# A linear-attention, mixture and maxout kernel: tile 1's loads and half of w_k moved up, the sums' writes later, first ffn mixing ahead of conversions

## The chip, the cores and the metric

The kernel runs on one core of one Trainium2 chip. The metric is the time of one execution on the device in microseconds; lower is better. The program has one launch, and all its weights and inputs are read from the chip's memory in it.

## The reference

Three stages follow one another over 3072 tokens of width 256. The first is a linear attention with a decaying state, in chunks of 32 in the reference; the second mixes each token with the one before it and runs a gated feed-forward layer; the third takes the largest of three products and projects it back.

```python
def _attn_ref(x, a, B, C):
    log_a = np.log(np.clip(a, 1e-06, 1.0))
...
    for c in range(nc):
...
        M = np.einsum('bhin,bhjn->bhij', Cc, Bc) * L
        y_intra = np.einsum('bhij,bhjd->bhid', M, xc)
        y_inter = np.einsum('bhin,bhnd->bhid', Cc, state) * decay_to_i[:, :, :, None]
        y[:, :, sl] = y_intra + y_inter
        state = decay_full[:, :, None, None] * state + np.sum(Bx, axis=2)

def _moe_ref(x, mu_k, mu_r, w_k, w_v, w_r):
...
    xk = mu_k * x + (1.0 - mu_k) * x_prev
    xr = mu_r * x + (1.0 - mu_r) * x_prev
    k = np.maximum(xk @ w_k, 0.0)
    v = k * k @ w_v
    r = 1.0 / (1.0 + np.exp(-(xr @ w_r)))
    return (r * v).astype(np.float32)

def _moe2_ref(x, w1, w2, w3, w_out):
    h = np.maximum(np.maximum(x @ w1, x @ w2), x @ w3)
    return (h @ w_out).astype(np.float32)
```

The weights come as 64-bit floats, and the kernel makes each product of a large layer as three products of split numbers (high by high, low by high, high by low).

## The kernel before

The 768 positions of four sequences are cut into six tiles of 128 positions; a tile has 512 tokens. `attention(t)` works on two chunks of 64 positions in each tile. For a tile it does the following. `inputs(t)` loads bl (B) and xt (x) and multiplies bl with a decay into bd. `gather` (L770) forms what each chunk adds to the state, from bd and xt; `heads` masks it into um. `cb` (L856) makes the scores of C (cw) and B (bt), which VectorE multiplies with the decays in L. `carried` (L881) multiplies the state with ce and `yt` (L891) the scores with xt, both into the accumulators pb0 and pb1. Copies of these into xb (L929) end the tile's attention. `sums()` makes running sums of log a for all tiles with L599, copies them on ScalarE (L603 as they are, L604 through exp), and writes them to memory as crd and ced, from where later tiles read the rows L and ec that `decays` and the state need. For tiles 0 and 1 the decays are spread on TensorE instead (L716 to L724).

`gate(t)` mixes xb with the token before it (L961, L962, L964), splits the result into k2h and k2l (L413 and L421, the high and the low part) and multiplies with w_r (L982), and `ffn(t)` mixes with the other weights into xk00h, xk00l, xk01h and xk01l, multiplies with w_k in eight groups of six products (L1005), squares the positive part on ScalarE (evacuations L1011, L1012, L1014), and multiplies with w_v (L1026). `maxout` (L686 on) and `final` follow for the tile before.

`load_split` brings a block of 64-bit weights: one DMA, an Abs on ScalarE (L629), four bit operations on VectorE (L630 to L636), a copy of the high part and a subtraction for the low part. wrh, wrl, wkh, wkl, wvh and wvl are the results. The first half of w_k comes as two blocks, the second half as one into h2, converted by way of wol.

What sets the order is the class `Plan`. Every operation is entered with a cost, its readers and writers, and a `bias`; a list scheduler in the kernel's own Python simulates the five engines 60 times with urgencies taken from the last round, and `issue()` writes each engine's instructions in the order of the best round. An engine works its list strictly in order. All loads go through one list, SyncE's. `first` adds to the bias of a DMA alone, `after` names operations that must come before. The planner has constants for what it knows of the chip: FETCH, BLOCK and FRONT say when TensorE's next block of instructions is there, EARLY is a number of very narrow matmuls (L1165) put ahead of all work, and WARM rules fillers (L1163) between.

## Time and profile before

| what | us |
|---|---|
| runs | 414.48, 414.15, 410.01 |
| median | 414.15 |
| profiled execution | 413.59 |
| its span, from first to last instruction | 411.9 |
| TensorE busy | 400.0 |
| VectorE busy | 254.8 |
| ScalarE busy | 215.3 |
| GpSimd busy | 62.3 |

The mean granted clock of TensorE is 0.987 of the full one. The chain of work that ended last runs through TensorE for 83% of the span, through VectorE for 8%, ScalarE 4%, DMA 2%, and "issue" (time in which an engine waits for nothing that the profile shows) 2%. Matmul lengths in the timeline overlap the next ones: in a row of 128x512 products one starts 0.23 us after another, whatever their listed lengths say. Line numbers of the profile are those of the kernel before; in the changed kernel they are 1 to 6 higher.

### The profile page before, as it was taken

How to read it: one execution, taken by the hardware profiler on the slowest of the kernel's cores; microseconds unless marked ns; L12 is line 12 of the kernel's file. 1: busy time of each engine (PE TensorE's matmuls, PEld its weight loads, DVE VectorE, ACT ScalarE, POOL GpSimd, SP SyncE). 2: the span in 40 equal slices, each digit the busy share in tenths (PEclk: the TensorE clock that was granted, in tenths of full speed). 3: DMA queues.
4: the chain of work that ended last, by engine and by line, in shares of the span. 5: the costliest groups of instructions: out<-in, count | busy, mean ns of one | idle time of the engine just before them, and what ended most of it. 6: DMA issues, size and time to landing. Idle time of an engine off the chain costs nothing.

```text
span 411.9 us, 8673 instructions
## 1 busy us (share of the span) xinstructions
PE 400.0 (97%) x3687; PEld 320.8 (78%) x3687; DVE 254.8 (62%) x413; ACT 215.3 (52%) x379; POOL 62.3 (15%) x63
## 2 busy tenths in 40 slices
PE   9797999999999999999999999999999999999996
PEld 6565777878877888787888888888887888888885
DVE  3898989999998655473664474565374224540632
ACT  5499578974476843255762154762145743222321
POOL 4104010000102340232130032140022200010010
PEclk9999799999999999999999999999999999999999
DMA  7686637560135500023300000500000000001001
GB/s 270 226 244 206 216 100 209 180 204 26 55 96 178 138 25 0 29 79 115 91 25 2 28 2 4 127 25 0 2 2 27 0 25 2 0 0 53 0 2 51
DMA packets 12879, 31.55 MB, mean 77 GB/s; under 512 B 1768, under 2 KB 4136, under 8 KB 12072
## 3 DMA queue, kind: packets, MB, share of 16 engines
q1 hardware_dynamic: 12840, 30.99, 24.3%
q8 instruction: 29, 0.48, 0.5%
q14 instruction: 10, 0.08, 0.1%
HBM read 27.64 MB, written 3.34 MB: 75 GB/s over the span
## 4 chain that ended last, share of the span: by engine, by line
PE 83%; DVE 8%; ACT 4%; issue 2%; DMA 2%; SPq 0%; ACTq 0%
PE pa L686 31%; PE pa L1026 15%; PE pa L1005 14%; PE pa L1102 9%; PE pa L982 3%; PE pb L1102 2%; PE pb L891 2%; PE pb L856 2%; DVE tmp L1064 1%; PE pb L881 1%; PE pa L701 1%; DMA bl<-in_b_l_dram 1%; PE pa L1165 1%; DVE tmp L964 1%; DMA outs<-in_w_out_dram 1%
## 5 line engine op out<-in xcount | busy, mean ns | idle before, releaser
L1064 DVE TENSOR_TENSOR tmp<-tmp,pa 128x512 f32<-128x512 f32 x72 | 49.1, 686 | 55.6 <-PE pa L686 54.6
L421 DVE TENSOR_TENSOR k2l<-tmp,k2h 128x512 fp32r<-128x512 f32 x52 | 37.5, 735 | 41.2 <-ACT tmp L1014 33.9
L413 ACT ACTIVATE hr<-tmp 128x512 fp32r<-128x512 f32 x36 | 22.7, 632 | 70.7 <-DVE tmp L1064 70.5
L1026 PE MATMUL pa<-k2h,wvh 128*128 128x512 f32 x96 | 38.2, 398 | 0.0
L1026 PE MATMUL pa<-k2h,wvl 128*128 128x512 f32 x96 | 38.0, 396 | 0.0
L1026 PE MATMUL pa<-k2l,wvh 128*128 128x512 f32 x96 | 37.8, 393 | 0.0
L1102 PE MATMUL pa<-hr,worh 128*128 128x512 f32 x120 | 37.5, 394 | 0.0
L1011 ACT ACTIVATE tmp<-pa 128x512 f32<-128x512 f32 x48 | 28.0, 593 | 13.9 <-PE pa L1005 13.6
L1062 ACT ACTIVATE tmp<-pa 128x512 f32<-128x512 f32 x36 | 21.5, 598 | 23.1 <-PE pa L686 19.4
L1012 ACT ACTIVATE k2h<-tmp 128x512 fp32r<-128x512 f32 x48 | 30.2, 632 | 2.9 <-PE pa L1026 1.6
L421 DVE TENSOR_TENSOR hr<-tmp,hr 128x512 fp32r<-128x512 f32 x28 | 19.3, 695 | 14.8 <-ACT hr L413 14.7
L421 POOL TENSOR_TENSOR hr<-tmp,hr 128x512 fp32r<-128x512 f32 x8 | 10.3, 1291 | 110.9 <-ACT hr L413 110.9
L1102 PEld LDWEIGHTS pa<-hr,worh 128*128 128x128 f32 x120 | 22.2, 188 | 5.5 <-ACT th L987 0.7
L1014 ACT ACTIVATE tmp<-tmp 128x512 f32<-128x512 f32 x37 | 23.3, 633 | 0.7
L1102 PE MATMUL pa<-hr,worl 128*128 128x512 f32 x60 | 23.4, 389 | 0.0
L1026 PEld LDWEIGHTS pa<-k2h,wvh 128*128 128x128 f32 x96 | 18.0, 188 | 4.4 <-issue 0.2
L1026 PEld LDWEIGHTS pa<-k2h,wvl 128*128 128x128 f32 x96 | 18.0, 188 | 4.3
L1026 PEld LDWEIGHTS pa<-k2l,wvh 128*128 128x128 f32 x96 | 18.0, 188 | 4.1
L1073 ACT ACTIVATE outs<-pa 128x512 f32<-128x512 f32 x9 | 5.4, 599 | 26.5 <-PE pa L1102 26.5
L964 DVE SCALAR_TENSOR_TENSOR tmp<-xb,bits,tmp 128x512 f32<-128x512 f32 x24 | 18.4, 792 | 0.7 <-ACT tmp L962 0.3
L868 DVE TENSOR_TENSOR L<-pb,L 128x512 f32<-128x512 f32 (+1 forms) x28 | 15.8, 608 | 2.7 <-ACT h L629 2.6
L1041 DVE SCALAR_TENSOR_TENSOR tmp<-th,pa 128x512 f32<-128x512 f32 x12 | 8.0, 689 | 14.5 <-PE pa L1026 14.5
(273 smaller groups left out, 986.5 us busy)
## 6 DMA issues: line engine op xcount, KB each, us to landing
h<-in_w_dram SPq DMA_DIRECT2D x6, 768.0 KB, 5.0
L<-crd SPq DMA_DIRECT2D x8, 512.0 KB, 6.6
cw<-in_c_w_dram SPq DMA_DIRECT2D x6, 512.0 KB, 4.0
xt<-in_x_l_dram SPq DMA_DIRECT2D x6, 512.0 KB, 3.5
out_dram<-outs SPq DMA_DIRECT2D x10, 256.0 KB, 2.0
h<-in_w_v_dram SPq DMA_DIRECT2D x2, 1024.0 KB, 6.0
bt<-in_b_t_dram SPq DMA_DIRECT2D x6, 256.0 KB, 4.4
bl<-in_b_l_dram SPq DMA_DIRECT2D x6, 256.0 KB, 3.5
```

The source lines that it names most:

```text
L413: A.activation(ap(out_), ap(in_), AF.Copy)
L421: op({"DVE": tt(n), "POOL": pool(n, narrow)}, 0, lambda e: (V if e == "DVE" else G).tensor_sub(ap(out_), ap(x0), ap(x1)), r=r, w=w, after= ...
L686: T.matmul(pt, l, r_, start=(i == 0), stop=(i == last))
L964: op("DVE", 61 + tt(n), lambda tv=tv, c=c: V.scalar_tensor_tensor(out=tv, in0=xb[:, c, bs, :P], scalar=om[:, i, c:c + 1], in1=tv, op0=ALU. ...
L1005: T.matmul(p.ap[:, :n], l, r_, start=(c == 0 and i == 0), stop=(c == KC - 1 and i == 2))
L1011: op("ACT", 51 + 0.833 * n, lambda: A.activation(sq, p.ap[:, :n], AF.Relu), r=[p], w=[tm])
L1012: op("ACT", act(n), lambda: A.activation(hi, sq, AF.Square), r=[tm], w=[kb])
L1014: A.activation(sq, sq, AF.Square) if e == "ACT" else
L1026: T.matmul(pv[c2].ap[:, :n], l, r_, start=(f == 0 and i == 0), stop=(f == FC - 1 and i == 2))
L1062: op("ACT", 51 + 0.833 * TW, lambda p=p, tm=tm: A.activation(tm.ap, p.ap, AF.Copy), r=[p], w=[tm])
L1064: op("DVE", tt(TW), lambda p=p, tm=tm: V.tensor_tensor(out=tm.ap, in0=tm.ap, in1=p.ap, op=ALU.max), r=[p], w=[tm])
L1102: T.matmul(p.ap, l, r_, start=(g == 0 and i == 0), stop=(g == GC - 1 and i == 2))
```

## The change

There are five edits. The planner's second FETCH entry now ends at 14.5 us with a delay of 2.8 us in place of 20 and 3.4, and EARLY is 140 where it was 118. The writes of crd get a bias that puts them behind those of ced. The first half of w_k and the mixing of the first ffn get a bias of 40000, which makes them more urgent. The second half of w_k and the loads of tile 1 (bl, xt, bt, cw) no longer follow one another by `after`: the chain was bt, w_k, cw, ct, then bl and xt, and now each of them waits for one thing, the first gather of tile 0, and ct for nothing, with biases that give them the order w_k, bl, xt, bt, cw, ct.

```diff
--- before.py
+++ after.py
@@ -91,11 +91,11 @@
     FIRST = 1500.0
     STAY = 8000.0
     BLOCK, FRONT = 128, 92
-    FETCH = ((9000.0, 5600.0), (20000.0, 3400.0), (60000.0, 3200.0), (1e9, 2600.0))
+    FETCH = ((9000.0, 5600.0), (14500.0, 2800.0), (60000.0, 3200.0), (1e9, 2600.0))
     OPEN = (1000.0, 28.0)
     HEAVY = (2100.0, 16000.0, 1300.0)
     WARM = (3400.0, 430.0, 215.0, 100.0, 600.0)
-    EARLY = 118
+    EARLY = 140
     ROUNDS = 60
     SPARE = (200.0, 1000.0)
     ENGINES = ("PE", "ACT", "POOL", "DVE", "SP")
@@ -337,6 +337,7 @@
 SPREAD = 2
 LATE = 0
 EARLY1 = -20000.0
+AHEAD = (40000.0, 40000.0)
 FIRST = (9.85e5, 9.8e5, 9.9e5, 9.83e5, 9.5e5, 9.95e5, 9.6e5)
 
 
@@ -605,7 +606,7 @@
         for s in range(2):
             dma(200, ced[s * QH:(s + 1) * QH], crow[:, s, 1], r=[b_er], w=[b_ced[s]])
             dma(200, crd[:, s * QH:(s + 1) * QH].rearrange("c q i -> q c i"),
-                crow[:, s, 0].rearrange("q (c i) -> q c i", c=2), r=[b_cr], w=[b_crd[s]])
+                crow[:, s, 0].rearrange("q (c i) -> q c i", c=2), r=[b_cr], w=[b_crd[s]], first=EARLY1)
         p = boot.bufs[2]
         op("PE", 350, lambda p=p: T.matmul(p.ap[:, :NC], tri, la, start=True, stop=True), r=[b_la, b_tri], w=[p])
         b_cc.readers = [k for s in (b_af, b_ts) for k in s.readers + s.writers]
@@ -652,18 +653,20 @@
         plan.bias = BIAS[1]
         load_split(w_r.rearrange("p (k n) -> p k n", k=KC), wr_t[0], wr_t[1], KC, CH, [b_wr], FIRST[3],
                    place=(stage.next(2 * TW), word.next(TW)))
-        plan.bias = 0.0
+        plan.bias = AHEAD[1]
         spots = [(stage.next(2 * TW), word.next(TW)), ((wo_f[0][:, :2 * TW], wide[:1]), word.next(TW)),
                  (stage.next(4 * TW), (wo_f[1][:, :2 * TW], narrow[:1]))]
         for c in range(KC):
             load_split(w_k[c * P:(c + 1) * P, None, fs[0]], wk_t[0][:, c:c + 1, fs[0]], wk_t[1][:, c:c + 1, fs[0]],
                        1, FF // 2, [b_wk[c][0]], FIRST[4] - 1.5e5 * c, place=spots[c])
-        k = dma(935, bt.rearrange("p u i -> p (u i)"), b_t[1], w=[b_bt], first=FIRST[4] - 4e5)
-        k = load_split(w_k[:, fs[1]].rearrange("(c p) n -> p c n", p=P), wk_t[0][:, :, fs[1]], wk_t[1][:, :, fs[1]],
-                       KC, FF // 2, [b_wk[c][1] for c in range(KC)], FIRST[4] - 4.5e5, place=spots[2], after=[k])
-        k = dma(1870, cw.rearrange("p u i -> p (u i)"), c_w[1], w=[b_cw], after=[k])
-        k = dma(935, ct.rearrange("p u i -> p (u i)"), c_t[1], w=[b_ct], after=[k])
-        inputs(1, after=[k])
+        plan.bias = 0.0
+        k = [begun['loads']]
+        load_split(w_k[:, fs[1]].rearrange("(c p) n -> p c n", p=P), wk_t[0][:, :, fs[1]], wk_t[1][:, :, fs[1]],
+                       KC, FF // 2, [b_wk[c][1] for c in range(KC)], FIRST[4] - 4e5, place=spots[2], after=k)
+        inputs(1, (FIRST[4] - 4.2e5, FIRST[4] - 4.3e5), after=k)
+        dma(935, bt.rearrange("p u i -> p (u i)"), b_t[1], w=[b_bt], first=FIRST[4] - 4.4e5, after=k)
+        dma(1870, cw.rearrange("p u i -> p (u i)"), c_w[1], w=[b_cw], first=FIRST[4] - 4.5e5, after=k)
+        dma(935, ct.rearrange("p u i -> p (u i)"), c_t[1], w=[b_ct], first=FIRST[4] - 4.6e5)
         for f in range(FC // 4):
             load_split(w_v[f].rearrange("p (k n) -> p k n", k=4), wv_t[0][:, 4 * f:4 * f + 4], wv_t[1][:, 4 * f:4 * f + 4], 4, CH, [b_wv[f]])
 
@@ -823,10 +826,11 @@
 
         def states(k):
             m = 32 * len(k)
-            op("PE", m * 10.8 + SWITCH * m / 64, lambda: gather(t, U, k), r=[b_bd, b_xt[t]], w=[U[c] for c in k], burst=m)
+            begun['states'] = op("PE", m * 10.8 + SWITCH * m / 64, lambda: gather(t, U, k), r=[b_bd, b_xt[t]], w=[U[c] for c in k], burst=m)
 
         if t < 2:
             states((0,) if first else (0, 1))
+            begun.setdefault('loads', begun['states'])
 
         def heads(c):
             uv = U[c].ap[:, TW // 2:].rearrange("p (b s d) -> p b s d", b=NB, s=2)
@@ -991,7 +995,9 @@
     def ffn(half, t):
         hv, cols, bs, n = tokens(half)
         xkt, b_xkt = xk_hl[t % 2], b_xk[t % 2]
+        plan.bias += AHEAD[0] * (t == 0)
         mix(0, xkt, b_xkt, half, t)
+        plan.bias -= AHEAD[0] * (t == 0)
 
         def s2(f):
             p = pm.next()
```

On SyncE's list this stood before from the load of tile 1's bt on (ced, crd: the sums; h2 and h3: weights; xt0, xt1: x of even and odd tiles):

```order
L426 DMA woh_79<-in_w_k_dram 128x1024
L426 DMA bt_115<-in_b_t_dram 128x512
L426 DMA h2_93<-in_w_k_dram 128x2x1024
L426 DMA xt0_121<-in_x_l_dram 128x1024
L426 DMA ced_82<-h0_91 96x128 x2
L426 DMA h3_94<-in_w_v_dram 128x2048
L426 DMA cw_116<-in_c_w_dram 128x1024
L426 DMA ec_119<-ced_82 128x1x512
L426 DMA ct_117<-in_c_t_dram 128x512
L426 DMA crd_81<-h0_91 96x2x64 x2
L426 DMA bl_124<-in_b_l_dram 128x512
L426 DMA xt1_122<-in_x_l_dram 128x1024
```

And now:

```order
L427 DMA woh_79<-in_w_k_dram 128x1024
L427 DMA h2_93<-in_w_k_dram 128x2x1024
L427 DMA bl_124<-in_b_l_dram 128x512
L427 DMA xt1_122<-in_x_l_dram 128x1024
L427 DMA bt_115<-in_b_t_dram 128x512
L427 DMA cw_116<-in_c_w_dram 128x1024
L427 DMA ct_117<-in_c_t_dram 128x512
L427 DMA xt0_121<-in_x_l_dram 128x1024
L427 DMA h3_94<-in_w_v_dram 128x2048
L427 DMA ced_82<-h0_91 96x128
L427 DMA crd_81<-h0_91 96x2x64
L427 DMA ced_82<-h0_91 96x128
```

bl and xt1 of tile 1 have moved from behind both writes of the sums to behind the second half of w_k, and the next x (xt0) and w_v stand ahead of the sums as well.

On ScalarE, from the copy of tile 0's result into xb on to the splits for the gate (k2h0 and k2h1), there stood before:

```order
L929 ACTIVATE xb0_129<-pb0_135 128x4x128
L604 ACTIVATE h0_91<-pa3_134 96x2x128
L612 ACTIVATE ccol_64<-pa2_133 128x192
L962 ACTIVATE tmp1_108<-xb0_129,bits_128 128x512
L962 ACTIVATE tmp2_109<-xb0_129,bits_128 128x512
L962 ACTIVATE tmp3_110<-xb0_129,bits_128 128x512
L413 ACTIVATE wkh_67<-h1_92 128x512
L413 ACTIVATE k2h0_99<-tmp0_107 128x512
L413 ACTIVATE k2h1_101<-tmp1_108 128x512
L629 ACTIVATE wol_80<-h2_93 128x1024
```

And now, from the copy of the sums on:

```order
L604 ACTIVATE h0_91<-pa3_134 96x2x128
L414 ACTIVATE wkh_67<-h1_92 128x512
L933 ACTIVATE xb0_129<-pb1_136 128x4x128
L613 ACTIVATE ccol_64<-pa2_133 128x192
L630 ACTIVATE wol_80<-h2_93 128x1024
L966 ACTIVATE tmp1_108<-xb0_129,bits_128 128x512
L966 ACTIVATE tmp2_109<-xb0_129,bits_128 128x512
L966 ACTIVATE tmp3_110<-xb0_129,bits_128 128x512
L926 ACTIVATE xb1_130<-xb0_129 128x8
L414 ACTIVATE k2h1_101<-tmp1_108 128x512
L735 ACTIVATE L_120<-pb0_135 128x8x64
L414 ACTIVATE k2h0_99<-tmp0_107 128x512
```

The conversion of the second half of w_k (wol), one evacuation of the spread (L735) and the small copy of xb have moved ahead of k2h0, and both copies of the sums stand ahead of xb.

On TensorE, at the gather of tile 1 (L770 before, L773 now; pa0 and pa1 are the accumulators of the w_k groups) there stood before:

```order
L1005 MATMUL pa0_131<-xk01l_86,wkh_67 128x512
L1005 MATMUL pa0_131<-xk01h_85,wkl_68 128x512
L770 MATMUL pb0_135<-xt1_122,bd_125 32x64 x32
L856 MATMUL pb0_135<-cw_116,bt_115 64x128 x2
L856 MATMUL pb1_136<-cw_116,bt_115 64x128 x2
```

And now:

```order
L1011 MATMUL pa0_131<-xk01l_86,wkh_67 128x512
L1011 MATMUL pa0_131<-xk01h_85,wkl_68 128x512
L773 MATMUL pb0_135<-xt1_122,bd_125 32x64 x32
L1011 MATMUL pa1_132<-xk00h_83,wkh_67 128x512
L1011 MATMUL pa1_132<-xk00l_84,wkh_67 128x512
```

Before, the gather comes behind the fourth group of w_k products and the scores right behind it; now it comes behind the first group, and the scores (L860) 12 products later, behind the third.

## Rows read from the trace of the kernel before

**Rows 1.** Page of the profile, busy time of each engine.

```profile
PE 400.0 (97%) x3687; PEld 320.8 (78%) x3687; DVE 254.8 (62%) x413; ACT 215.3 (52%) x379; POOL 62.3 (15%) x63
```

**Rows 2.** Busy times in stretches: busy us (instructions) by engine, PEclk, DMA share, GB/s.

```profile
70.00:120.00 50.00, 50.00 (x518) 40.54 (x517) 49.97 (x87) 36.39 (x66) 1.06 (x1) 1.00 0.35 108
```

**Rows 3.** Timeline of TensorE, 15 to 70 us: start, length, line, tiles, idle before.

```profile
18.01 0.71 PE L891 MATMUL pb<-L,xt 64*32 64x64 f32 x47 [2.26 <-issue]
...
19.60 1.17 PE L599 MATMUL pa<-tri,la 128*96 128x128 f32 x4
...
59.07 0.78 PE L891 MATMUL pb<-L,xt 64*32 64x64 f32 x55 [0.98 <-issue]
...
68.94 0.50 PE L1005 MATMUL pa<-xk10h,wkh 128*128 128x512 f32 x1 [0.57 <-ACT tmp L1011]
```

**Rows 4.** Busy times in stretches from the start, with counts of matmuls.

```profile
0.00:12.90 12.90, 11.89 (x221) 7.67 (x225) 6.48 (x19) 6.78 (x12) 4.59 (x24) 1.00 0.82 285
0.00:15.76 15.76, 14.74 (x350) 10.16 (x350) 9.31 (x25) 9.38 (x18) 5.48 (x25) 1.00 0.85 305
0.00:54.70 54.70, 48.35 (x861) 36.01 (x865) 43.99 (x74) 38.46 (x70) 13.04 (x29) 0.91 0.67 221
0.00:58.09 58.09, 51.74 (x988) 38.62 (x988) 46.41 (x77) 40.70 (x73) 13.04 (x29) 0.91 0.66 220
```

**Rows 5.** Busy times by microsecond; PEclk, DMA share and GB/s stand last.

```profile
13.00:14.00 1.00, 1.00 (x82) 0.91 (x71) 0.97 (x2) 0.90 (x3) 0.00 (x0) 1.00 1.01 410
18.00:19.00 1.00, 0.99 (x63) 0.90 (x67) 0.46 (x1) 0.00 (x0) 0.00 (x0) 0.92 0.00 0
19.00:20.00 1.00, 1.00 (x29) 0.88 (x23) 0.25 (x1) 0.31 (x1) 0.00 (x0) 0.50 0.34 70
22.00:23.00 1.00, 1.00 (x5) 0.40 (x3) 1.00 (x2) 1.00 (x3) 0.00 (x0) 0.87 0.36 98
40.00:41.00 1.00, 1.00 (x48) 1.00 (x49) 1.00 (x2) 0.89 (x2) 0.00 (x0) 0.50 1.04 434
46.00:47.00 1.00, 1.00 (x5) 0.78 (x5) 0.64 (x2) 0.50 (x2) 0.00 (x0) 0.93 1.05 362
59.00:61.00 2.00, 1.93 (x60) 1.66 (x61) 1.73 (x4) 1.25 (x3) 0.00 (x0) 1.00 0.17 25
```

**Rows 6.** Timeline of TensorE at the gate of tile 0.

```profile
24.70 0.50 PE L982 MATMUL pa<-k2h,wrh 128*128 128x512 f32 x1 [0.41 <-ACT k2h L413]
25.43 0.50 PE L982 MATMUL pa<-k2l,wrh 128*128 128x512 f32 x1 [0.22 <-DVE k2l L421]
```

**Rows 7.** Timeline of TensorE at the gather and scores of tile 1.

```profile
36.79 0.85 PE L770 MATMUL pb<-xt,bd 64*32 64x64 f32 x64 [0.29 <-DMA xt<-in_x_l_dram]
39.79 2.01 PE L856 MATMUL pb<-cw,bt 32*64 32x128 f32 x64 [2.15 <-ACT um L777]
```

**Rows 8.** Timeline of SyncE's queue, DMA issues of 10 to 32 us.

```profile
10.82 0.43 SPq L426 DMA_DIRECT2D h<-in_w_k_dram  x1
...
31.02 0.83 SPq L426 DMA_DIRECT2D crd<-h  x2
```

**Rows 9.** Timeline of VectorE at tile 1's bd.

```profile
35.40 1.08 DVE L761 TENSOR_TENSOR bd<-bl,dfj 128x512 f32<-128x512 f32 x1 [1.20 <-DMA bl<-in_b_l_dram]
```

**Rows 10.** Timeline of TensorE at the start.

```profile
1.00 3.31 PE L1165 MATMUL pa<-sbd 128*32 128x16 bf16 x118 [1.00 <-DVE xb L559]
...
5.72 1.91 PE L701 MATMUL pa<-tmp,ccol 128*128 128x512 f32 x2
```

**Rows 11.** Chain of waits, 20 to 27 us: start, length, step.

```profile
21.45 0.33 ACT ccol L612
21.78 1.83 ACT tmp L962 x3
...
24.13 1.04 ACT k2h L413 x2
25.17 1.02 ACT wol L629
```


## The prediction

> **What bounds the kernel now.** I read the busy times first, then the chain of waits, then TensorE's timeline up to 70 us, and last the granted clock in stretches. TensorE is busy for 400.0 us of a span of 411.9 [rows 1], and from 70 to 120 us it does not rest at all [rows 2]. VectorE is just as full there (49.97 of 50.00 us), so it may take over whenever TensorE comes early. A gain has to come from the time before 70 us in which TensorE waits or runs at the lower clock. The ledger of that time:
>
> - It stops for 2.26 us ahead of 18.01, in the intra-chunk products of tile 0, and for 0.98 ahead of 59.07, both released by "issue" [rows 3]. 350 matmuls had run by 15.76 and 988 by 58.09 [rows 4]. The planner's constants expect an edge between instruction blocks at 92 + 128n products, which gives 348 and 988, so I read both stops as a block of instructions that was not there yet. The edge ahead of the first was passed at 12.90 (221 matmuls), that of the second at 54.70 (861) [rows 4]: from passing an edge to running the next block took 5.1 and 4.4 us, the first time with the DMA engines full [rows 5].
> - After the first stop the granted clock is 0.92 of 2.4 GHz, three times 0.50 (the level of 1.2 GHz) and 0.87 in successive microseconds [rows 5]: 0.08 + 3 x 0.50 + 0.13 = 1.7 us, of which I count 1.6, since not every product there is bound by the clock.
> - The gate products wait 0.41 and 0.22, together 0.63 us, for k2h and k2l [rows 6].
> - The gather of tile 1 waits 0.29 us for xt at 36.79, and its scores wait 2.15 us for um at 39.79: 2.44 [rows 7]. The chain behind it starts at SyncE: crd waits for the sums on ScalarE and leaves at 31.02, and bl and xt of tile 1 stand behind it in one queue [rows 8]. VectorE's bd waits 1.20 us for bl up to 35.40 [rows 9]; VectorE's and ScalarE's um follow.
> - After that wait the clock is 0.50 for six microseconds, then 0.93 [rows 5]: 6 x 0.50 + 0.07 = 3.1 us.
> - The second fetch stop is 0.98, a wait for an evacuation 0.57 at 68.94 [rows 3].
>
> Sum: 2.26 + 1.6 + 0.63 + 2.44 + 3.1 + 0.98 + 0.57 = 11.6 us.
>
> **The change part by part.**
>
> **Loads of tile 1.** bl and xt1 now stand right behind the second half of w_k, which waits only for the first gather, and ahead of every crd and ced. That half left at 10.82 [rows 8]; the first gather, into which the 221st matmul falls, runs at 12.9 [rows 4], so bl and xt leave near 13.5 in place of 32 or so. The w_k half and the five loads behind it are 2.75 MB by their shapes; at the 0.4 MB per us of [rows 5] they take 7 us, and bl and xt, the first of the five, land by about 18. The 2.44 us go, and with them the 3.1 at 1.2 GHz: the gather now stands behind the first of the w_k groups and the scores behind the third, so 12 x 0.23 us of other products cover the chain of bd and um, two operations of about 1 us. What is late next there is the evacuation of those groups (below). Gain: 5.5. On SyncE ced and crd now wait for the sums with ec(1), bl(2) and the second half of w_v behind them. The second scan ends with the products at 59.07 [rows 3], and the sums are there by 21 (below), so this costs nothing; its cover is some 25 us, and without it the scan would wait as the scores did, 2.15.
>
> **Narrow matmuls.** 22 more, at 3.31/118 = 28 ns [rows 10], are 0.6 us. The first L701 pair took 1.91 us where later ones take 1.02: if those reach the full rate at the same time as now, half comes back. Bounds 0 and 0.6; I take 0.3.
>
> **First fetch stop.** All edges move 22 products forward. Edge 220 falls on the first gather product, passed near 12.8, and edge 348 in the second gather, reached at about 15.7. With the 5.1 us of before the block is there at 17.9: a stop of 2.2 us. More load waits ahead of that block than before (2.75 MB where bt and the w_k half made 1.25), and 4.4 us were enough at 54.70: bounds 1.5 and 2.9 (0.7, the difference of the two, to either side). The 5.1 is for the same edge under the same full engines, so 2.2 stays, with 1.6 of clock behind it. The rows show stops at exactly these edges. The Trainium skill ("Runtime: NRT & Kernel Launch", Instruction fetch mechanics) says that instructions come in blocks of 16 KiB, 256 instructions, that the next is fetched while the current one runs, and that a crossing is mostly hidden. The block agrees with 128 matmuls and their weight loads in [rows 4]; the hiding disagrees with the 2.26 us in [rows 3]. By that rule the sum would be that of the first rival.
>
> **Sums and carried products.** L600 (before, L599: 1.17 us at 1.2 GHz [rows 3]) is now ahead of the carried products, and 72 of the products behind the stop take 72 x 0.71/47 = 1.1. So y is complete at 17.9 + 1.1 + 1.2 + 1.0 = 21.2, where it was 19.7. These products are only moved: no cost but for those who wait for y.
>
> **The chain to the gate.** This is what takes the place of the removed wait. ScalarE does, in order, two copies of the sums (after L600, from 20.4), wkh, xb, ccol, the wol conversion, three L966, a small copy of xb, k2h1, one L735 and only then k2h0, which the gate takes first. In before wol and both L732 stood behind k2h. By the steps of [rows 11] (0.33 for ccol, 1.83 for the three, 1.04/2 for any 128x512, 1.02 for wol; 0.33 for each sum copy as for ccol, 0.2 for the small one): 20.4 + 0.66 + 0.52 + 0.52 + 0.33 + 1.02 + 1.83 + 0.2 + 0.52 + 0.52 + 0.52 = 27.0, and with 0.3 to start, 27.3. TensorE has L611, two fillers and the first spread in front. Between the end of L599 at 20.8 and the gate's wait at 24.3 [rows 3, 6] the first and the last took 3.5 us, a part of it at 1.2 GHz; with two fillers of a quarter of a microsecond each I put the whole at 3.8: 25.0. It waits 2.3 us where it waited 0.63. The waits of 2.26 and 2.15 were each followed by 0.50, the 0.98 was not (the clock of 59 to 61 us is 1.00, [rows 5]); I take a second drop at the price of the first, 1.6 us (bounds 0 and 3.1).
>
> **Second fetch stop.** Between the edges 860 and 988 now lie f2 and f3, six more products of 0.23 us than before: 1.4 us of cover against 0.98. As the edges shift by 24 products (22 narrow, two fillers), I keep 0.3 (bounds 0 and 0.98).
>
> **Order of ScalarE in the first two ffn.** Conversions of about 1.02 us and more stand ahead of evacuations of the w_k groups at four or five places. A group takes 6 x 0.23 = 1.36 us and its evacuation some 0.9 from the group's end, so with two buffers such a conversion costs up to 0.6. Five would be 3.0. In before similar places cost 0.57 in all [rows 3]. I take 1.8, the middle.
>
> **GpSimd and VectorE.** wkl goes to GpSimd, wrl to VectorE. Neither is wanted before the gate and the w_k groups; nothing, bounds 0 and 0.5, one such 128x512 step.
>
> After: 0.3 + 2.2 + 1.6 + 2.3 + 1.6 + 0.3 + 1.8 = 10.1, which is 1.5 less than 11.6. The profiled execution took 413.59 us, 1.7 more than its span and 0.6 less than the median of 414.15. 413.59 - 1.5 = **412.1 us**.
>
> **The rivals.**
>
> No fetch stop at 15.7. For it: the planner's constant for a block begun before 14.5 us becomes 2.8 us, with which it is there at 15.6. Against: 5.1 in the trace. Without the stop and its clock loss 3.8 go, but the chain to the gate comes only some 3 us earlier, so 0.8 come back: 409.1. The rule of the Trainium skill above gives this time.
>
> The gate wait without 1.2 GHz behind it. For it: the clock has just come back up at that time, and 0.98 us of rest did nothing. Against: 2.15 and 2.26. 412.1 - 1.6 = 410.5.
>
> VectorE takes over. From 70 to 120 us it is full, and it gets wrl besides. If it has no lead there, TensorE waits for it as much as it came earlier: 413.6. Against: in before TensorE waited for nothing in those 50 us.
>
> The long gate chain, slower than before. If the wait at the gate is followed by the long stretch (3.1 in place of 1.6), ScalarE's order costs its upper 3.0 and the first stop its 2.9: 412.1 + 1.5 + 1.2 + 0.7 = 415.5. It decides at the gate: 1.5 us more there, by waiting or by clock, and the gain is gone.
>
> Tile 1's loads come no earlier, because one of them waits on SyncE for something of tile 0. The 5.5 stay and the new losses come on top: 417.6. Against: in the order nothing but the first gather, bd and the scores of tile 0 stands ahead.
>
> **How the numbers follow.** Chances: forecast 0.38 (its own range 411 to 414), no 1.2 GHz at the gate 0.15, no fetch stop 0.17, VectorE 0.12, long gate chain 0.14, loads late 0.04. The range for 8 in 10 takes in the forecast, the two faster rivals with 0.3 to spare and most of the long chain: 408.8 to 416.0. One per cent, 4.1 us, is about what a measurement of this kernel can tell from no change; one of the three runs of before lies that far below the others. Faster by over 1% (under 409.5 to 410) holds 0.10 of the first rival, 0.05 of the second and 0.07 of the forecast with its terms at their lower bounds: 0.22. Slower by over 1% (over 417.7): half of the late loads and 0.06 of the long chain, 0.08. Within: 0.70.
>
> **What would show it.** Right: no wait of the gather for xt or of the scores for um in tile 1, and full clock behind them; "issue" of 2 us near 15.7; a gate wait of over 2 us, released by ScalarE's k2h, with clock 0.50 behind it; several short waits for evacuations L1017. Wrong: no "issue" there, a gate that starts before 26, or a VectorE that releases TensorE between 70 and 120 us.

## The result, and the profile after

The changed kernel takes 415.65 us (median of 22 runs, 411.34 to 420.88), the kernel before beside it 412.62 (22 runs, 409.70 to 414.85). The ratio is 1.0062 [1.0033, 1.0091]: slower by 0.6%, 2.6 us, where the forecast was 1.5 us faster. All ratios here leave out the runs that lie over 1.5% above the fastest of their kernel (the profiled execution of e4_wol, below, with 420.08 us is one), so they are not the quotients of the medians. The profiled execution took 416.55 us with a span of 414.8; before, 413.59 and 411.9. Line numbers are those of the changed kernel. Its page of busy times:

```profile
PE 400.7 (97%) x3711; PEld 320.9 (77%) x3711; DVE 256.8 (62%) x418; ACT 215.0 (52%) x375; POOL 63.1 (15%) x61
```

TensorE has 0.7 us more to do [rows 1] in a span 2.9 longer, so the rest is waiting, or a lower clock elsewhere than before. Its timeline from 15 to 80 us, the waits and the two places at which it waited before:

```profile
17.66 0.32 PE L773 MATMUL pa<-xt,bd 64*32 64x64 f32 x3 [2.38 <-issue]
...
27.15 0.50 PE L986 MATMUL pa<-k2h,wrh 128*128 128x512 f32 x1 [1.23 <-ACT k2h L414]
27.87 0.50 PE L986 MATMUL pa<-k2l,wrh 128*128 128x512 f32 x1 [0.23 <-DVE k2l L422]
...
34.63 0.86 PE L773 MATMUL pb<-xt,bd 64*32 64x64 f32 x64
...
38.40 1.21 PE L860 MATMUL pb<-cw,bt 32*64 32x128 f32 x64
...
49.98 0.86 PE L773 MATMUL pb<-xt,bd 64*32 64x64 f32 x64 [0.53 <-DVE bd L764]
...
56.97 1.02 PE L895 MATMUL pb<-L,xt 64*32 64x64 f32 x79 [1.41 <-issue]
...
68.81 0.50 PE L1011 MATMUL pa<-xk10h,wkh 128*128 128x512 f32 x1 [0.73 <-ACT tmp L1017]
...
74.22 0.50 PE L1011 MATMUL pa<-xk10h,wkh 128*128 128x512 f32 x1 [2.39 <-ACT tmp L1017]
```

The gather (34.63) and scores (38.40) of tile 1 wait for nothing now; they cost 2.44 us [rows 7]. The first stop is 2.38 where it was 2.26, the second 1.41 where it was 0.98 [rows 3]. New are the wait at the gate, one of 0.53 for tile 2's bd, and above all 0.73 and 2.39 for evacuations of tile 1's w_k groups. The clock, in stretches (the granted clock is third from the end, before DMA share and GB/s):

```profile
17.00:18.00 1.00, 0.34 (x26) 0.34 (x32) 1.00 (x3) 0.05 (x1) 0.00 (x0) 0.58 1.03 404
18.00:23.00 5.00, 5.00 (x106) 3.71 (x88) 3.03 (x5) 3.23 (x8) 1.64 (x2) 0.50 1.00 349
23.00:24.00 1.00, 1.00 (x3) 0.40 (x3) 1.00 (x2) 1.00 (x3) 1.00 (x1) 0.51 0.92 311
36.00:60.00 24.00, 22.07 (x394) 17.53 (x393) 22.84 (x33) 20.72 (x37) 8.40 (x1) 1.00 0.49 166
75.00:76.00 1.00, 1.00 (x4) 0.78 (x3) 1.00 (x3) 1.00 (x3) 0.00 (x0) 0.59 0.04 16
76.00:78.00 2.00, 2.00 (x6) 1.54 (x6) 2.00 (x4) 1.47 (x3) 0.00 (x0) 0.50 0.66 102
78.00:79.00 1.00, 1.00 (x5) 0.83 (x4) 1.00 (x3) 0.07 (x1) 0.00 (x0) 0.70 0.56 209
```

The long stretch at 1.2 GHz that stood from 40 to 46 us [rows 5] is gone: 36 to 60 us run at 1.00. But the one behind the first stop now costs 0.42 + 5 x 0.50 + 0.49 = 3.41 us where it cost 1.7, and a new one behind the 2.39 costs 0.41 + 1.00 + 0.30 = 1.71. With all clock counted, the ledger of before is 12.0 us (2.26 + 1.71 + 0.63 + 2.44 + 3.41 + 0.98 + 0.57), that of after 14.0 (2.38 + 3.41 + 1.46 + 0.53 + 1.41 + 0.73 + 2.39 + 1.71). The clock takes 5.12 us in both, at other places; what grew are the waits. These 2.0 us, 0.3 of waits behind 100 us (0.66 at 140.53, where before had 0.32 at 131.44) and 0.43 for two fillers ahead of the gate (0.85 us at the 0.50 that the 3.41 has counted already), less 0.43 by which the first gather comes earlier, make 2.3 of the 2.9; 0.6 us I did not find.

Who makes the evacuations late? ScalarE has the conversions of w3 and of the second half of w1 ahead of them, and they wait for loads (ScalarE's timeline):

```profile
67.37 0.91 ACT L630 ACTIVATE h<-h 128x768 f32<-128x768 f32 x1 [0.34 <-DMA h<-in_w_dram]
...
72.28 0.89 ACT L630 ACTIVATE wd<-h 128x768 f32<-128x768 f32 x1 [2.51 <-DMA h<-in_w_dram]
```

These loads stand on SyncE behind ec, which waits for a product on GpSimd (timelines of SyncE's queue and of GpSimd, all between 18 and 100 us of the latter):

```profile
60.00 0.61 SPq L427 DMA_DIRECT2D ec<-ced  x1
60.66 0.45 SPq L427 DMA_DIRECT2D xt<-in_x_l_dram  x1
61.21 3.71 SPq L427 DMA_DIRECT2D h<-in_w_dram  x2
64.97 1.14 SPq L427 DMA_DIRECT2D L<-crd  x2
```

```profile
21.36 1.27 POOL L422 TENSOR_TENSOR wkl<-h,wkh 128x512 fp32r<-128x512 f32 x1 [5.51 <-ACT wkh L414]
22.59 1.51 POOL L764 TENSOR_TENSOR bd<-bl,dfj 128x512 f32<-128x512 f32 x1
51.57 8.40 POOL L788 TENSOR_TENSOR sbd<-sbd,ec 128x256 f32<-128x256 f32 x1 [27.48 <-PE pb L885]
```

The product (tile 1's second state) stands there for 8.40 us; the same product took 0.62 us for tile 0. It ends at 59.97, and ec leaves at 60.00. VectorE works without a gap up to 59.48 and then rests for the first time (its timeline):

```profile
21.78 1.40 DVE L635 SCALAR_TENSOR_TENSOR wd<-woh,wd 128x512 uint32<-128x512 uint32 x1
23.10 1.28 DVE L965 TENSOR_SCALAR tmp<-xb,bits 128x512 f32<-128x512 f32 x1
...
58.52 0.96 DVE L635 SCALAR_TENSOR_TENSOR wd<-h,wd 128x768 uint32<-128x768 uint32 x1
60.31 1.41 DVE L968 SCALAR_TENSOR_TENSOR tmp<-xb,bits,tmp 128x512 f32<-128x512 f32 x2 [0.82 <-ACT tmp L966]
```

So the product ended 0.5 us after VectorE's first pause. It works the other way as well: beside GpSimd's wkl and bd, two VectorE steps ahead of the gate take 1.40 and 1.28 us where they took 0.69 and 0.48 (VectorE's timeline, kernel before):

```profile
20.69 0.48 DVE L961 TENSOR_SCALAR tmp<-xb,bits 128x512 f32<-128x512 f32 x1
...
23.09 0.69 DVE L634 SCALAR_TENSOR_TENSOR wd<-woh,wd 128x512 uint32<-128x512 uint32 x1
```

### The profile page after: what moved, and what is told of

The parts are those of the page before. It is cut to its first block, busy times and chain, and to the rows that moved or that the text cites. A ratio compares the mean times of both kernels' runs of the same rounds, so it can differ in the third digit from the quotient of the medians.

```text
span 414.8 us, 8732 instructions
## 1 busy us (share of the span) xinstructions
PE 400.7 (97%) x3711; PEld 320.9 (77%) x3711; DVE 256.8 (62%) x418; ACT 215.0 (52%) x375; POOL 63.1 (15%) x61
## 4 chain that ended last, share of the span: by engine, by line
PE 75%; DVE 13%; ACT 4%; DMA 3%; issue 3%; ACTq 0%; SPq 0%
PE pa L689 30%; PE pa L1032 12%; PE pa L1011 10%; PE pa L1108 9%; PE pa L986 3%; PE pb L1108 2%; DMA h<-in_w_dram 2%; PE pb L895 2%; DVE tmp L1070 2%; DMA outs<-in_w_out_dram 2%; PE pb L885 1%; DVE tmp L968 1%; DVE wd L637 1%; DVE k2l L422 1%; PE pa L1171 1%
## 5 line engine op out<-in xcount | busy, mean ns | idle before, releaser
L422 DVE TENSOR_TENSOR k2l<-tmp,k2h 128x512 fp32r<-128x512 f32 x54 | 39.0, 732 | 42.3 <-ACT tmp L1020 34.5
L1020 ACT ACTIVATE tmp<-tmp 128x512 f32<-128x512 f32 x35 | 22.0, 635 | 0.7
L968 DVE SCALAR_TENSOR_TENSOR tmp<-xb,bits,tmp 128x512 f32<-128x512 f32 x24 | 17.3, 747 | 1.2 <-ACT tmp L966 0.8
```

The lines of the kernel that those rows point to most:

```text
L422: op({"DVE": tt(n), "POOL": pool(n, narrow)}, 0, lambda e: (V if e == "DVE" else G).tensor_sub(ap(out_), ap(x0), ap(x1)), r=r, w=w, after= ...
L968: op("DVE", 61 + tt(n), lambda tv=tv, c=c: V.scalar_tensor_tensor(out=tv, in0=xb[:, c, bs, :P], scalar=om[:, i, c:c + 1], in1=tv, op0=ALU. ...
L1020: A.activation(sq, sq, AF.Square) if e == "ACT" else
```

## The experiments

Letters in the expectations stand for theories. The first was that ScalarE's order costs what the prediction had too little for (A). Its rivals put the loss before 30 us, at the first stop and the gate (B; D says that two chains set the gate), or put it down to what the conversions wait for, SyncE's order (C) and behind it GpSimd (E), or to the narrow matmuls. All kernels were timed in 5 rounds beside the kernel before, in groups in which its median was 412.3 to 413.2 us; so runs are compared by their ratios. "Waits" is what TensorE waits at evacuations in tile 1's ffn, 62 to 80 us, in the profiled execution.

| run | median us | ratio to before | waits us |
|---|---|---|---|
| e0_after | 415.98 | 1.0052 [1.0007, 1.0098] | 3.25 |
| e1_conv | 416.4 | 1.0084 [1.0049, 1.0120] | 2.25 |
| e2_rows | 414.21 | 1.0049 [1.0011, 1.0086] | 1.34 |
| e5_w3 | 413.02 | 1.0026 [0.9998, 1.0055] | 0.29 |
| g1_vec | 413.49 | 1.0010 [0.9978, 1.0043] | 0.28 |
| g2_vec_rows | 413.33 | 1.0023 [0.9993, 1.0053] | 0.29 |
| g3_rest | 412.84 | 1.0023 [0.9989, 1.0057] | 0.57 |
| e4_wol | 415.1 | 1.0058 [1.0020, 1.0096] | 5.04 |
| e6_pool | 416.0 | 1.0062 [1.0028, 1.0095] | 2.90 |
| e9_gate | 414.27 | 1.0039 [1.0007, 1.0072] | 2.55 |
| e7_both | 413.07 | 1.0012 [0.9981, 1.0044] | 0.49 |
| f3_mended | 411.7 | 0.9983 [0.9952, 1.0014] | 0.29 |
| e8_loads | 408.86 | 0.9915 [0.9885, 0.9945] | 0.61 |
| e11_loads_urgent | 410.47 | 0.9955 [0.9921, 0.9989] | 0.20 |
| e10_loads_early | 413.22 | 1.0015 [0.9985, 1.0045] | 2.29 |
| e12_loads_mix | 413.08 | 1.0019 [0.9990, 1.0047] | 0.36 |
| f1_after118 | 415.29 | 1.0061 [1.0025, 1.0098] | 3.57 |
| f2_loads140 | 409.44 | 0.9915 [0.9890, 0.9940] | 0.65 |

**The waits in tile 1's ffn.** e0_after is the changed kernel again. 

> The changed kernel again, beside the others of this group. Theory A (ScalarE's queue is blocked at 69.8 to 72.3 us by the conversion of a weight block whose load is late, and TensorE waits 2.39 us and then runs at 1.2 GHz for some 3 us) and theory B (the loss is made before 30 us: a low stretch of 6 us in place of 4 behind the first fetch stop, and 1.46 us of waits at the gate in place of 0.63) both expect what was measured: 0.6% slower than before, about 415 us.

 The two waits are there with 1.53 and 1.72, and the gate waits 1.95, which this time is followed by a stretch of 1.7 us at the lower clock; the one behind the first stop is 1.70.

e1_conv moves one conversion on ScalarE. The planned times stay; only the order in which instructions are written changes, here and in the next kernels:

```diff
+        at = list(start)
         for i in sorted(range(len(ops)), key=lambda k: (start[k], k)):
+            at[i] = max([start[i] + self.later.get(i, 0.0)] + [at[d] for d in ops[i][2]])
+        for i in sorted(range(len(ops)), key=lambda k: (at[k], start[k], k)):
...
+    plan.later = {plan.conv[9]: 5000.0}
```

> Only the Abs of the second half of w1 is moved eight places down ScalarE's list, behind four evacuations; loads and TensorE's order stay. Theory A: the wait of 2.39 us near 74 us and the 1.2 GHz behind it (1.7 us of loss) vanish, the time falls by 3.5 to 4 us against the changed kernel of this group, to 411 to 412, ratio to before 0.996 to 0.999. Theory B: nothing before 63 us is touched, so the time stays at 1.006.

 The second wait is gone, but the first grew to 2.25 (ScalarE waits 1.87 for the load of w3), and several of 0.2 to 0.7 followed later. The time did not fall: the place of this one conversion by itself is not the cause.

e2_rows puts the two L<-crd of tile 2 behind the later loads on SyncE.

```diff
+    plan.later = {k: 12000.0 for k in plan.rows[:2]}
```

> Only the two DMAs that spread the sums of tile 2 (L from crd) are issued two weight loads later on SyncE; ScalarE's order stays as in the changed kernel. Theory A with the share of the DMA engines as its cause: the load of the second half of w1 lands in about 5 us in place of 7.7, ScalarE's wait for it falls from 2.5 to under 0.5, and 3 to 4 us are won, 411.5 to 412.5. If the load is late for another reason, it still takes over 7 us and the time stays at 415. Theory B: no change, 415.

 The second wait is gone, the first stays at 1.34 (w3's conversion waits 0.96 for its load). So the rows delay the load of w1: it took 7.7 us from issue to landing in after, and 5.2 here. By its ratio the time cannot be told from that of e0_after. e5_w3 also brings w3 ahead of ec (387) and xt (413).

```diff
+    plan.later = {387: 2420.0, 413: 480.0, **{k: 12000.0 for k in plan.rows[:2]}}
```

> The changed kernel with SyncE's list mended: the load of w3's first half goes ahead of ec and xt of tile 2, behind which it stood until 61 to 63 us, and the two spreads of the sums go two weight loads later, as in the run before. Theory C (ScalarE's list holds conversions ahead of evacuations, and w3 and w1's second half are late because SyncE's list holds w3 behind ec, which waits for GpSimd, and because the spreads share the DMA engines): w3 leaves at about 58, both waits of ScalarE for loads near 70 to 74 us vanish, TensorE's waits between 66 and 77 fall from 3.2 us to under 0.8, and the time is some 2.5 to 3 us under the changed kernel, 412.5 to 413.5. Theory B (the loss is made before 36 us): 415 to 416, whatever the waits at 70 us do, since VectorE sets the pace behind them.

 Both are gone (0.29 is left), and the ratio is half of what it was above 1 (1.0026), though the intervals overlap. What the waits cost is the lateness of two loads, not ScalarE's order by itself.

The last three ask why ec is late. g1_vec has GpSimd's long product made by VectorE:

```diff
     plan.arrange()
+    plan.where[297] = "DVE"
```

> The changed kernel with one instruction moved to another engine: the product of tile 1's second state (sbd with ec, 128x256), which GpSimd takes 8.40 us for, from 51.57 to 59.97, is made by VectorE. Theory E: it is GpSimd's long product that holds ec on SyncE (it left at 60.00), and with it xt and the loads of w3 and of the second half of w1 behind it. Then ec leaves at 54 to 56, w3 at 58 to 60 where it left at 61.2 to 63, and the conversion of w3 no longer waits for its load; TensorE's wait at 68 to 71 us (0.73 and 1.53 in two executions of the changed kernel) goes below 0.4. The rows of L<-crd still leave right behind the second half of w1, so the second wait (1.72 and 2.39) stays at 1 to 2.4. Time 414.3 to 415.3, 0.7 to 1.7 under 415.98. The rival, that w3 is late by its own buffer or by the rows of L alone: no wait changes by more than 0.3, time 415.5 to 416.5.

 The timelines of VectorE, SyncE and TensorE in g1_vec:

```profile
55.51 0.42 DVE L794 TENSOR_TENSOR sbd<-sbd,ec 128x256 f32<-128x256 f32 x1
```

```profile
55.95 0.61 SPq L432 DMA_DIRECT2D ec<-ced  x1
59.02 0.32 SPq L432 DMA_DIRECT2D xt<-in_x_l_dram  x1
59.46 6.47 SPq L432 DMA_DIRECT2D h<-in_w_dram  x2
```

```profile
69.37 0.51 PE L1017 MATMUL pa<-xk10h,wkh 128*128 128x512 f32 x1 [0.28 <-ACT tmp L1023]
```

ec leaves as soon as the product is there, w3 at 59.46 (in the two executions of the changed kernel it left at 61.21 and 63.11), and both waits are gone: more than expected, since the second went too, though the rows of L still leave behind w1. One instruction on another engine does what e5_w3 does by hand. g2_vec_rows adds the later rows of e2_rows:

```diff
+    plan.where[297] = "DVE"
+    plan.later = {**{k: 12000.0 for k in plan.rows[:2]}}
```

> The move of g1_vec, and the two rows of L<-crd of tile 2 behind the later loads on SyncE, as in e2_rows. By theory E both waits at the evacuations of tile 1's ffn are gone without any load being moved by hand, and the time is that of e5_w3: 412.7 to 413.6. If it needs w3 ahead of ec for another reason, one wait of 0.7 or more is left and the time is that of e2_rows, 414 or more.

 It is no better than g1_vec: once ec is early, the rows harm nothing. g3_rest leaves the product on GpSimd and has VectorE wait for it, with a copy of one column of its result ahead of operation 144:

```diff
+            if i == self.rest_at:
+                self.rest()
...
+    plan.rest = lambda: V.tensor_copy(pause, sbd[:, 0, 0, 0, :1])
...
+    plan.rest_at = 144
```

> The changed kernel, with GpSimd's product left where it is, and one instruction more on VectorE: a copy of one column of the product's result, three bit operations after the place at which GpSimd begins, so that VectorE waits for GpSimd there. If GpSimd's 8.40 us are a standing aside for VectorE, which works without a gap from 51 to 59.5, the product ends within 1.5 us of VectorE's wait, some 5 us earlier than without, at about 55.5 to 56.5, VectorE waits 0.6 to 1.3, ec leaves right behind, and the waits and the time are those of g1_vec, within 0.8. If the 8.40 are the product's own or only a way in which the record shows it, it ends as late as before, VectorE waits 3 to 5 us and the time is 417 or more.

 The timelines of GpSimd and of VectorE in g3_rest:

```profile
53.18 3.65 POOL L797 TENSOR_TENSOR sbd<-sbd,ec 128x256 f32<-128x256 f32 x1 [28.78 <-PE pb L894]
```

```profile
55.67 0.68 DVE L430 TENSOR_TENSOR k2l<-tmp,k2h 128x512 fp32r<-128x512 f32 x1
56.87 0.15 DVE L1182 COPY pause<-sbd 128x1 f32<-128x1 f32 x1 [0.52 <-POOL sbd L797]
```

With a wait of 0.52 us on VectorE, GpSimd is done at 56.83, 0.5 us after VectorE stops, in place of 8.4 us after its own start, and the waits and the time go down as in g1_vec. GpSimd had been standing aside: theory E holds. The Trainium skill ("SBUF — State Buffer", SBUF: two separate sides) says that VectorE operations with two inputs from SBUF and GpSimd share one pair of ports as a lock, and that the second of them waits in full. The traces agree (8.40 us against 0.62), and show more: between VectorE instructions that follow one another, GpSimd did not get in for 7.8 us.

**The gate.** e4_wol moves the wol conversion behind k2h0 on ScalarE; e6_pool lets GpSimd begin wkl and bd (92, 111) only when k2l0 is there; e9_gate does both.

```diff
+    plan.later = {plan.conv[3]: 6000.0}
...
+    plan.hold_pool = lambda: G.tensor_copy(pause, xr_hl[0][1][:, :1].bitcast(F32))
...
+    plan.later = {92: 11000.0, 111: 2300.0}
...
+    plan.later = {92: 11000.0, 111: 2300.0, plan.conv[3]: 6000.0}
```

> Only the Abs of the second half of w_k (wol, 1.02 us) is moved behind k2h0 on ScalarE, so the gate of tile 0 may start. Theory A: the gate starts some 0.8 to 1.0 us earlier and its wait falls from 1.46 to about 0.5, but the block at 72 us remains: 414 to 414.5, ratio 1.003 to 1.004. Theory B: the gate is a main part of the loss, and with it goes at least 1.0, with the low stretch unchanged: 413.5 to 414; A and B differ here by little.

 

> The changed kernel with GpSimd held: a copy of one column of k2l0 stands ahead of wkl and bd on GpSimd, so that these two run behind the mixing for the gate and not beside it. Theory B (wkl and bd on GpSimd stretch VectorE's bit operation from 0.69 to 1.4 us and its mixing step from 0.48 to 1.3, which makes the gate wait 2.2 us and the clock fall behind it): the gate starts about 1.5 us earlier, near 26.0, its wait falls to 0.5 to 0.9, no 1.2 GHz behind it, 3 us won, 412.5 to 413. If ScalarE sets the gate, nothing changes (415 to 416).

 

> The changed kernel with both hindrances of the gate taken away: GpSimd held until k2l0 is there, and ScalarE's Abs for wol moved behind k2h0. Theory D (two chains set the gate, VectorE's mixing beside GpSimd and ScalarE's list with wol in it, and either alone keeps it late): the gate starts 7.5 to 8.0 us after the first fetch stop ends, where it was 8.9 to 9.1 with one or none of them taken away; its wait falls to about 1.0, the clock does not fall behind it in most executions, and the time is 1 to 3 us under the changed kernel, 412.5 to 414.5. If a third thing sets it (y itself, or the sums), it stays at 8.9 and 415 to 416.

 In e4_wol ScalarE then waits 1.12 for VectorE, and the gate still 2.30. In e6_pool VectorE's steps are back at 0.68 and 0.48 but it waits 0.91 for ScalarE, and from the end of the first stop to the gate it is 8.86 us, in e0_after 8.96. With both it is 7.97; TensorE's and VectorE's timelines in e9_gate:

```profile
25.62 0.50 PE L995 MATMUL pa<-k2h,wrh 128*128 128x512 f32 x1 [1.23 <-ACT k2h L422]
```

```profile
21.68 0.68 DVE L643 SCALAR_TENSOR_TENSOR wd<-woh,wd 128x512 uint32<-128x512 uint32 x1
22.28 0.48 DVE L974 TENSOR_SCALAR tmp<-xb,bits 128x512 f32<-128x512 f32 x1
```

Two chains of about the same length end at the gate, ScalarE's with wol and VectorE's beside GpSimd, so either alone mends nothing. What the mended gate is worth in time is not shown: 1.0039 for e9_gate against 1.0052, with intervals that overlap. e7_both (e5 and e6) and f3_mended (e4, e5 and e6 together) add up the mends.

```diff
+    plan.later = {387: 2420.0, 413: 480.0, **{k: 12000.0 for k in plan.rows[:2]}, 92: 11000.0, 111: 2300.0}
...
+    plan.later = {387: 2420.0, 413: 480.0, **{k: 12000.0 for k in plan.rows[:2]}, 92: 11000.0, 111: 2300.0, plan.conv[3]: 6000.0}
```

> Both mends at once. If B and C are two separate losses, they add: 5 to 6 us under the changed kernel, 410 to 411, and 1.5 to 2.5 under before, ratio 0.994 to 0.996. If VectorE is the limit from 63 to 130 us, the second mend brings nothing on top of the first: 412.5 to 413.

 

> The changed kernel with all mends: GpSimd held until k2l0, the Abs for wol behind k2h0, w3 ahead of ec on SyncE, the spreads of the sums later. If the two losses add, the gate's 1.0 to 1.5 us with the 1.7 behind it and some 3 us at 66 to 77, it is 4 to 5.5 us under the changed kernel, 410.5 to 412, and under before. If VectorE takes back what the gate gives, 413, as with the SyncE mend alone.

 e7_both is as fast as e5_w3 alone (413.07 and 413.02 us), so the two mends did not add; holding GpSimd without moving the wol conversion had mended nothing in e6_pool either. f3_mended is 0.7% under e0_after by the ratios, 2.8 us, and cannot be told from the kernel before.

**The parts of the change.** e8_loads is the kernel before with the edit of tile 1's loads alone (the second half of w_k and the five loads behind it, and `begun['states']`; no bias, FETCH, EARLY or crd edit). The crd edit leaves the order of every engine as it is, alone and on top of the other four, so it has no run; that the writes of crd and ced stand otherwise in the new list of SyncE is the work of the other edits.

```diff
+        k = [begun['loads']]
...
+        inputs(1, (FIRST[4] - 4.2e5, FIRST[4] - 4.3e5), after=k)
```

> Before with one part of the change alone: the new waits and order of the second half of w_k and of tile 1's loads; no other edit. The planner makes an order of its own for it. If the loads themselves are the gain (2.44 us of waits and 3.1 at 1.2 GHz of before are gone) and the losses come from the other edits, it is 2 to 4 us under before, 408.5 to 410.5. If the losses come with the loads (another order of ScalarE and GpSimd in which something else waits), it is within 1 us of before or slower.

 408.86 us (408.55 to 409.81) is the best time of all. TensorE's waits from 14 to 100 us in e8_loads, all of them:

```profile
17.95 0.96 PE L894 MATMUL pb<-L,xt 64*32 64x64 f32 x47 [2.78 <-issue]
26.24 0.50 PE L985 MATMUL pa<-k2l,wrh 128*128 128x512 f32 x1 [0.31 <-DVE k2l L421]
40.35 0.50 PE L1008 MATMUL pa<-xk00h,wkh 128*128 128x512 f32 x1 [0.52 <-ACT tmp L1014]
65.26 0.50 PE L1008 MATMUL pa<-xk10h,wkh 128*128 128x512 f32 x1 [0.61 <-ACT tmp L1014]
```

There is no wait of the gather or the scores, no second stop, and tile 1's second state is not made on GpSimd in this order. The next three put other edits on top of e8_loads: FETCH and EARLY, both biases, and the mixing bias alone.

```diff
+    FETCH = ((9000.0, 5600.0), (14500.0, 2800.0), (60000.0, 3200.0), (1e9, 2600.0))
+    EARLY = 140
...
+        plan.bias = 40000.0
...
+        plan.bias += AHEAD[0] * (t == 0)
...
+        plan.bias += AHEAD[0] * (t == 0)
```

> The loads part of the change (408.9 us alone) and with it the planner's new FETCH entry and the 140 narrow matmuls; no other edit. If these spoil the gain, 412 to 415; if they cost only the narrow matmuls themselves, 0.3 to 0.6 us, it is 409 to 410.

 

> The loads part and with it both biases of 40000 (first half of w_k, mixing of the first ffn); FETCH and the 118 narrow matmuls as before. If the urgencies spoil the gain, because conversions for w_k and the ffn take ScalarE, VectorE and GpSimd ahead of the gate, 412 to 416; if not, 409 to 410.

 

> The loads part and with it the bias of the first ffn's mixing alone. If the mixing ahead of the gate is the part that spoils, as in the run with both biases, 412 to 416; if the bias of w_k is, 409 to 410 here.

 Each has lost something in another place (by the ratios e11_loads_urgent, 0.9955, is not clear of 0.9915): e10_loads_early waits 1.53 for xk00l at 33.70 and 1.87 at 71.02, e11_loads_urgent has a second stop of 2.61, e12_loads_mix waits 3.66 for wkl at 34.59. The changed kernel is e11_loads_urgent with FETCH and EARLY (and crd): that step costs 1.1% by the ratios, 0.9955 to 1.0062, some 4.4 us. Is it the narrow matmuls themselves, or the order that the planner makes with the new constants? f1_after118 keeps the order of the changed kernel and issues 118; f2_loads140 keeps that of e8_loads and issues 140.

```diff
     plan.arrange()
+    plan.EARLY = 118
...
     plan.arrange()
+    plan.EARLY = 140
```

> The changed kernel's order on every engine, with 118 narrow matmuls issued in place of 140. If the narrow matmuls themselves (0.6 us and the place of the block edges) spoil the gain, it falls by 2 to 5 us under the changed kernel, to 411 to 414; if the order that the planner makes of FETCH and EARLY does, it falls by at most 0.6 us: 415 to 416.

 

> The order of the kernel with the loads part alone (408.9 us), with 140 narrow matmuls issued in place of 118. If the narrow matmuls themselves spoil the gain, 411 to 414, as with FETCH and EARLY entered into the planner; if the planner's order does, 409 to 409.7.

 Neither changes the ratio: it is the order. The 22 narrow matmuls are worth 0.58 us by the medians (409.44 against 408.86), at most, and nothing by the ratios (0.9915 for both).

## Why the prediction was wrong, step by step

- **Tile 1's loads**: right. The waits and the long stretch behind them are gone, 2.44 + 3.41 (the forecast's 3.1 left out the part before 40 us); alone the edit gives 0.85% [0.55, 1.15], 3.5 us, with part given back at a longer first stop, 2.78 with 3.41 of clock behind it.
- **Narrow matmuls**: I took 0.3 of 0 to 0.6. In the profile of after nothing is left of them: the first pair of L704 ends at 7.64 us, where its counterpart ended at 7.63 [rows 10].
- **First fetch stop**: 2.2 forecast, 2.38 and 2.17 measured in the two executions. The rival without a stop fell, and with it the time by the Trainium skill's rule of a hidden crossing. Of the clock behind it I took 1.6; it was 3.41 and 1.70.
- **The chain to the gate**: 2.3 with 1.6 of clock forecast; 1.46 without in after, 2.18 with 1.7 in e0_after. In e0_after the size was right, in after TensorE came later itself, under the longer low stretch; and only half the cause was right: I gave it to ScalarE alone, and VectorE beside GpSimd is as long.
- **Second fetch stop**: 0.3 forecast with 0.98 as the upper bound; 1.41 and 1.27. The six products that were to cover it did not. In the eleven other profiled executions with this place of the stop (x79) it was 0.47 to 1.56, so 1.41 is not a growth over 0.98 that can be relied on.
- **Order of ScalarE in the first two ffn**: 1.8 (up to 3.0) forecast as five conversions of up to 0.6. Measured are 3.1 and 3.25, with 1.71 of clock in after, and the mechanism was another: two conversions, each waiting for its load.
- **GpSimd and VectorE: "nothing, bounds 0 and 0.5"**, and SyncE: "costs nothing". This is the step that failed: in place of nothing, GpSimd's 8.40 us and the queue of SyncE behind them made the loads late, and with them the evacuations, 3.1 us of waits with 1.71 of clock where the forecast had 1.8 in all. Mending it takes most of the loss away: without the 8.4 us (g1_vec, g2_vec_rows, g3_rest) the ratios are 1.0010, 1.0023 and 1.0023, and with them (the changed kernel twice, f1_after118) 1.0062, 1.0052 and 1.0061. That is 0.3 to 0.5%, 1.2 to 2.1 us; single intervals of the two sides overlap, but the three of the one side all hold 1 and the three of the other do not. I looked only at what GpSimd does for TensorE, not at who shares its time or what SyncE waits for. The trace of before had it, in a row that I did not weigh (timeline of GpSimd, kernel before):

```profile
16.11 0.80 POOL L785 TENSOR_TENSOR sbd<-sbd,ec 128x256 f32<-128x256 f32 x1
30.95 3.73 POOL L785 TENSOR_TENSOR sbd<-sbd,ec 128x256 f32<-128x256 f32 x1 [14.04 <-DMA ec<-ced]
```

The same product at 0.80 and 3.73 us: the second stood beside a VectorE that was busy up to 34.20, and ended 0.5 us later. SyncE stood behind GpSimd there too: its load of ct waited 2.3 us for the next GpSimd instruction, ce, and left as that ended (timelines of GpSimd and of SyncE's queue, kernel before).

```profile
34.63 1.29 POOL L845 TENSOR_TENSOR ce<-ct,ec 128x512 f32<-128x512 f32 x1
```

```profile
35.96 0.33 SPq L426 DMA_DIRECT2D ct<-in_c_t_dram  x1
```

- **The rivals**: the slower one, the long gate chain, gave 415.5, near the time, but this is luck: of its three terms only the 3.0 at the evacuations came, by another mechanism, while the gate had no long stretch and the first stop not its 2.9. VectorE did not take over between 70 and 120 us.

What stays open: why the second stop was not covered and spreads so widely, whether the 0.1 to 0.2% that g1_vec to g3_rest show over the kernel before are a loss, and which detail of the orders of e10_loads_early and e12_loads_mix costs most.

## What to carry to other kernels

An instruction on an engine "with time to spare" is not free: ask what it shares with a busy neighbour, and which queue waits for its end; one product on GpSimd stood for 8.4 us with the queue of loads behind it, and taking it away gave back 0.3 to 0.5% of the time. When several edits come together, time each alone: one was worth 3.5 us here, and the others cost more than that. In a kernel whose order a planner makes, a constant moves work in places that have nothing to do with it, so read the new order on the queue of loads as closely as on the busiest engine.

## What I had not expected of the hardware

GpSimd hardly got in between VectorE instructions that follow without a gap: 8.40 us for a product of 0.62, in ten profiled executions of nine kernels with that order within 0.01 us of one another. Each time it ended 0.48 us after VectorE's first rest, and a rest of 0.13 us was enough (f3_mended). In g3_rest it was 3.65. e7_both is the exception: the product took 4.52 us and ended at 58.07 without a rest of VectorE, where one VectorE instruction, on the result of a ScalarE conversion that had ended only at 57.47, took 0.98 us in place of 0.55:

```profile
57.51 0.98 DVE L639 TENSOR_SCALAR wd<-wd 128x768 f32<-128x768 f32 x1
```

So GpSimd took that place; why there and not at another the traces do not show.

The clock's low stretches came in two sizes: every one between 5 and 400 us, in all twenty profiled executions, cost 1.7 or 3.4 us (for instance 3.41 and 1.71 in after). Behind gate waits of 1.95 to 2.36 us a stretch followed in all eight profiled executions that had one, behind 1.23 to 1.88 in none of six. But elsewhere 2.25 us of rest had none (e1_conv, 71.78) and 1.87 had one (e10_loads_early, 71.02), so the length of the wait alone does not tell it.
